# One load for the first keys, the second sketch matrix on GpSimd's queue, two banks for the last output tile, and a new order of all steps

## The chip, the cores and the metric

The kernel runs on one NeuronCore of a Trainium2 chip. The metric is the device time of one execution in microseconds, the median of a few runs; lower is better. Five engines work side by side and meet only at semaphores: TensorE (PE, matmuls), VectorE (DVE), ScalarE (ACT), GpSimd (POOL) and SyncE (SP, which here only starts transfers). Each takes its instructions strictly in the order in which they are written for it.

## The reference

An attention with sketched polynomial features feeds a layer with a rational activation. S is 1,088, there are 4 batches and 4 heads of 32 dimensions, and the output is 4,352 tokens of 128 values.

```python
def phi(x):                                   # 32 -> 64 features
    a = einsum('rd,bhsd->bhsr', S1, x); b = einsum('rd,bhsd->bhsr', S2, x)
    return einsum('bhsi,bhsj->bhsij', a, b).reshape(*x.shape[:-1], 64)
q_p, k_p = phi(q), phi(k)
kv  = einsum('bhsf,bhsd->bhfd', k_p, v);  z = sum(k_p, axis=2)
att = einsum('bhsf,bhfd->bhsd', q_p, kv) / (einsum('bhsf,bhf->bhs', q_p, z)[..., None] + 1e-6)
x = att.transpose(0, 2, 1, 3).reshape(4352, 128)
h = x @ w_in                                  # 128 -> 2048
P = a0 + a1*h + a2*h**2 + a3*h**3;  Q = 1 + |b0|*|h| + |b1|*h**2
out = (P / (Q + 1e-6)) @ w_out                # 2048 -> 128
```

## The kernel before

The whole program is one list of short steps, `ORDER`, read from left to right. Each step emits a few instructions on one engine, and an engine's queue is what the list gives to it, so the list alone sets the order of work on each engine. A letter behind the last dot picks the engine where there is a choice (`a` ScalarE, `d` VectorE).

Keys, `K<b>.<step>` for batch b: `T0`, `T1`, `T2` transpose parts of the keys on VectorE (L299), `s0`/`s1` sketch them on TensorE (L306), `c` copies one sketch out of PSUM, `f` multiplies the two sketches into features on VectorE (L318), `p0`/`p1` multiply the features with the values (L337, 72 matmul records in all), `k` keeps the result in `kvz`.

Queries, `Q<b>.<y>.<step>` for chunk y of batch b (256 to 384 tokens): `T` transposes, `sk` sketches, `c` copies the sketch, `dw` and `dr` write it to device memory and read it back repeated (SP), `f` makes the features, `p` multiplies with `kvz` (L433), `pl`, `r`, `x` divide, `b` transposes back on TensorE, `kk` copies the tokens into the ring `xT`. The first two chunks of batch 0 go without `dw` and `dr`.

The layer works in 21 units, each a number of tokens (256 or 512) by a number of blocks of 128 hidden values (4, 8 or 16), most of them 128 x 4,096 values. For unit i: `H<i>.<part>` the first matmul into a pair of PSUM banks (L518), `E` the cast out of them (ScalarE mostly, L272), `U` the absolute value, `W` and `Y` the denominator on VectorE (L531, L539, L554), in some units `D` (ScalarE) with `M` (an adding transfer from GpSimd), `P` and `V` the numerator (L559, L572), `A` an adding transfer, `L` and `X` logarithm and exponential on ScalarE (L576, L581), which make the reciprocal, `S` and `G` the products with it (L585, L589), and `Or`, `Os`, `Og` (and `Om`, `On` in units 16 and 17) the second matmuls (L618), which add into an output tile. `ST` copies that tile out of PSUM, `OUT` stores it. The last 256 tokens are units 18, 19 and 20.

`F<b>.k`, `.q`, `.v` load the next batch, `I<n>` are the loads at the start, `SS0` makes the sketch weights from S1 and S2 on VectorE (with some on GpSimd), `w`, `KA`, `AB`, `RT` prepare the weights and coefficients of the layer, `AW0` writes a constant. `Z<n>` is n idle matmuls of 128 x 512 that compute nothing (L197).

In PSUM a pool `att` has three banks (`att_ps`), `hps` two pairs (`h_ps`), and `ops` a single bank, `out_ps`, in which every output tile is built in turn. So the first `Or` of a tile waits until `ST` of the tile before has copied it out. In SBUF two buffers `out_sb` take the copies in turn; those of units 16 and 20 share one.

At the start, ScalarE's queue loads S1; SP loads the first 4 of the 9 key columns of each quarter (`I0`), S2 (`I11`), the other 5 columns (`I1`), half of the queries (`I2`), the values (`I3`, four transfers) and the rest. At the end `turn_out` of unit 20 copies one half of the last tile with VectorE and the other with ScalarE, and SP and ScalarE store one half each.

Of the kernel before, what the change touches and what calls it, by code (L numbers as in the profile page):

```python
# [43 lines left out]
Q0.1.b K1.p0 K1.p1 E2.1.a Q1.0.c.a w5.a Q0.1.kk.a L0.0 P2.0.d Q0.2.f Q0.2.p Q0.2.pl.a K1.k0.a X0.0 Q1.2.T U2.0.d
Q0.2.r Q1.1.sk Q1.2.sk Q0.3.dw F2.k Q1.0.dw Q0.2.x Q0.2.b Or0.0 W2.0.d S0.0 V2.0 K2.T0 G0.0 Y2.0 Q0.2.kk.a L1.0
Q1.1.c.a X1.0 H3.0 E3.0.a H3.1 E3.1.a K2.s0 K2.c0.a H3.2 L2.0 Q1.2.c.a E3.2.a F2.q Q0.3.dr Q1.1.dw S1.0 K2.T1 P3.0.d
G1.0 Q2.0.T K2.f0 Q2.1.T H3.3 E3.3.a Q0.3.f U3.0.d K2.T2 W3.0.d Q2.2.T Y3.0 Os0.0 H4.0 H4.1 Og0.0 Q2.0.sk Q1.0.dr
Q1.2.dw Q1.1.dr K2.s1 Q0.3.p X2.0 E4.0.a P3.1.a H4.2 Q0.3.pl.d K2.c1.d Q1.0.f Q2.0.c.a E4.1.a Og1.0 Q0.3.r V3.0 Q1.0.p
Q0.3.x L3.0 Q1.0.pl.a Q1.2.dr H4.3 E4.2.a Os1.0 Q1.0.r E4.3.a Q1.0.x Q0.3.b Q0.3.kk.a Q1.0.b Or2.0 S2.0 U4.0.d
Q1.0.kk.a H5.2 K2.f1 Q1.1.f W4.0.d X3.0 Q2.0.dw H5.3 E5.3.a G2.0 Q2.1.sk F2.v Q2.2.sk Q2.1.c.a F3.q E5.2.a Q1.1.p Y4.0  # L50
Q2.2.c.a Q1.1.pl.a Q1.1.r H5.0 E5.0.a Og2.0 L4.0 H5.1 Q1.2.f Or1.0 H6.2 Q1.1.x S3.0 E5.1.a Os2.0 ST2.a E6.2.a P4.0.d
Q3.1.T H6.3 Q1.1.b E6.3.a X4.0 Q1.1.kk.a H6.0 E6.0.a U5.0.d H6.1 Q3.0.T Q3.0.sk Q2.1.dw Q3.0.c.a W5.0.d E6.1.a K2.p0
K2.p1 K2.k0.a D6.0 Q1.2.p V4.0 Y5.0 S4.0 F3.k K3.T2 K3.T1 H7.0 K3.T0 E7.0.a U6.0.d G3.0 M6.0 Q1.2.pl.a Os4.0 H7.2
Or4.0 L5.0 E7.2.a H7.3 Q2.0.dr Q2.0.f Q2.0.p Q1.2.r Q2.1.dr Q2.1.f Q3.0.dw Q1.2.x X5.0 P5.0.d Q3.0.dr Q2.2.dw Q1.2.b
Q1.2.kk.a E7.3.a H7.1 Og3.0 G4.0 Q2.0.pl.d Q3.2.T E7.1.a Q2.0.r H8.3 V5.0 Q2.0.x Q2.0.b S5.0 L6.0 H8.2 E8.2.a U7.0.d
E8.3.a F3.v Or3.0 Q2.0.kk.a P6.0.d W7.0.d P7.0.d H8.0 V6.0 Os3.0 X6.0 Y7.0 E8.0.a S6.0 H8.1 E8.1.a U8.0.d D8.0 Q2.2.dr
OUT2 Og4.0 ST4.a H9.0 Q3.1.sk Q3.1.c.d Q2.2.f Q2.1.p Q2.1.pl.d K3.s0 K3.c0.d Q2.1.r Q3.2.sk Q3.2.c.d E9.0.a H9.1 Or6.0
L7.0 M8.0 Q2.1.x Q2.1.b K3.f0 H9.2 E9.1.a X7.0 E9.2.a Os6.0 H9.3 E9.3.a V7.0 AW0 Or5.0 P8.0.d H10.3 G6.0 L8.0 G5.0
S7.0 U9.0.d E10.3.a W9.0.d H10.0 E10.0.a V8.0 Q3.1.dw Y9.0 Og6.0 X8.0 H10.1 H10.2 Og5.0 E10.1.a A7.0 G7.0 E10.2.a
Q2.1.kk.a H11.0 Q3.1.dr Q3.1.f Os5.0 S8.0 D10.0 Q2.2.p E11.0.a U10.0.d P9.0.d K3.s1 Q2.2.pl.d ST6.a Q3.2.dw H11.1  # L60
Or8.0 Q3.0.f OUT6 Q2.2.r H11.2 K3.c1.d Q2.2.x L9.0 E11.1.a P10.0.d Q2.2.b K3.f1 V9.0 M10.0 V10.0 X9.0 E11.2.a H11.3
E11.3.a S9.0 K3.p0 K3.p1 w7.d U11.0.d w6.d L10.0 W11.0.d H12.1 E12.1.a Or7.0 H12.0 K3.k0.d Q3.0.p Q3.1.p X10.0 Y11.0
Q3.1.pl.d H12.2 Q3.0.pl.a G8.0 E12.0.a L11.0 E12.2.a Q3.0.r Os8.0 A9.0 H12.3 E12.3.a Q3.1.r Og8.0 Q3.0.x Q3.0.b Og7.0
Q3.1.x G9.0 Q2.2.kk.a S10.0 A10.0 Q3.0.kk.d H13.0 D12.0 Q3.1.b Q3.1.kk.a U12.0.d ST8.a M12.0 P12.0.d H13.1 E13.1.a
Q3.2.dr P11.0.d E13.0.a Or9.0 X11.0 H13.3 Q3.2.f V12.0 G10.0 V11.0 S11.0 H13.2 E13.3.a E13.2.a U13.0.d Or10.0 H14.1
E14.1.d L12.0 OUT4 Q3.2.p W13.0.d Q3.2.pl.a Q3.2.r H14.2 E14.2.d H14.0 X12.0 E14.0.a H14.3 Q3.2.x Q3.2.b Y13.0 E14.3.a
Q3.2.kk.a H15.2 D14.0 S12.0 U14.0.d A12.0 G12.0 E15.2.a Og10.0 Og9.0 ST10.a P14.0.d Z4 H15.3 P13.0.d L13.0 A11.0
Or12.0 G11.0 V14.0 V13.0 E15.3.a X13.0 S13.0 H15.1 Og11.0 E15.1.a H15.0 E15.0.a Or11.0 M14.0 U15.0.d L14.0 H16.1
P15.0.d W15.0.d OUT8 E16.1.a H16.0 E16.0.a Og12.0 X14.0 H16.3 ST12.a E16.3.a V15.0 OUT10 Y15.0 H16.2 S14.0 E16.2.a
Or13.0 U16.0.d A13.0 OUT12 G13.0 W16.0.d H17.3 H17.1 L15.0 Og13.0 E17.3.a A14.0 G14.0 Y16.0 E17.1.a X15.0 H17.0  # L70
E17.0.a S15.0 H17.2 E17.2.a U17.0.d L16.0 W17.0.d Og14.0 Or14.0 ST14.a A15.0 G15.0 H18.0 X16.0 Y17.0 S16.0 H18.1
E18.1.a E18.0.a Or15.0 U18.0.d B16.0 W18.0.d C16.0 Og15.0 H19.0 L17.0 X17.0 Os16.0 E19.0.a Y18.0 S17.0 Or16.0 Om16.0
# [7 lines left out]
def kernel(  # L80
# [63 lines left out]
        eng.dma_start(out=t, in_=bass.AP(tensor=s_in.tensor, offset=s_in.offset, ap=[[0, 16], [D, R], [1, D]]))  # L144
# [15 lines left out]
    qT0 = [ln_sb[:, 2048 + QW * i:2048 + QW * (i + 1)] for i in range(2)]  # L160

    def early(n):
        if n == 11:
            s_raw.append(spread_s(nc.sync, 1, S2))
        elif n < 2:
            j, e = ((0, 4), (4, NT))[n]
            nc.sync.dma_start(out=k0.rearrange("p (m t d) -> p m t d", m=NM, d=D)[:, :, j:e],
                              in_=bass.AP(tensor=k.tensor, offset=k.offset + j * D,
                                          ap=[[NJ * D, 128], [NT * D, NM], [1, (e - j) * D]]))
# [433 lines left out]
    def gather(i, y, k):  # L603
        t0, tl, f0, n = units[i]
        first = t0 not in outs
        if first:
            outs[t0] = ops.tile([128, TC], FP, name="out_ps")
        c, ce = span(i, "LSGGG"[y], k)
        for j, x in enumerate(range(c // tl, ce // tl)):
            left[t0] -= 1  # L610
            z = (live[i]["s3", 0][:, x * tl:(x + 1) * tl] if y == 4
                 else at(i, "rsgg"[y], x * tl, (x + 1) * tl))
            w = w_sb[y][:, f0 + x, :]
            if not (TOK or t0 + tl == n_tok):
                nc.tensor.matmul(outs[t0][:, :tl], lhsT=w, rhs=z, start=first and j == 0, stop=left[t0] == 0)
                continue
            for m in range(tl // 128):
                nc.tensor.matmul(outs[t0][:, m * 128:(m + 1) * 128],  # L618
                                 lhsT=z[:, m * 128:(m + 1) * 128], rhs=w,
                                 start=first and j == 0 and m == 0, stop=left[t0] == 0 and m == tl // 128 - 1)  # L620

    def turn_out(i, eng="d"):
# [10 lines left out]
        nc.vector.tensor_copy(out=o[:, 0:128], in_=outs[t0][:, 0:128])  # L633
# [1 line left out]
        nc.scalar.copy(out=last, in_=outs[t0][:, 128:256])
# [135 lines left out]
```

## Time and profile before

| | us |
|---|---|
| median of three runs | 254.69 (254.11 to 255.16) |
| the profiled execution | 254.41 |
| its span, first to last instruction | 252.6 |
| PE busy | 244.7 (97%) |
| VectorE busy | 240.3 (95%) |
| ScalarE busy | 229.2 (91%) |
| GpSimd busy | 31.2 (12%) |

The profile is one execution of the program. Its page gives busy times of the engines, slices of the span, the chain of waits that ended last, and the costliest groups of instructions. Behind the page stands the trace, which can be asked for the timeline of an engine, for busy times in any stretch, or for one tile. A row of a timeline is start, duration, engine, line, operation and shapes, and in brackets the idle time before it and what ended it. A busy matmul row is a modelled one, and rows that overlap are merged.

### The profile page before, as it was taken

The page shows a single profiled execution, that of the slowest core. Times are in us where ns is not written, and L with a number is a line of the kernel's source. Part 1 is how long each engine was busy: PE and PEld are TensorE (multiplying, and loading weights), DVE is VectorE, ACT ScalarE, POOL GpSimd, SP SyncE. Part 2 cuts the span into 40 slices and gives each one's busy share as a digit, 9 for nine tenths or more (in the row PEclk, how much of TensorE's full clock was granted, in tenths as well). Part 3 has the DMA queues.
Part 4 walks back from the last instruction along what each step waited for, and adds up shares of the span by engine and source line. Part 5 has one row for each costly group of instructions (what it writes and reads, how often), then busy time and mean ns, then how long its engine had stood idle before and what let it go on. Part 6 is the DMA issues. An engine that isn't in the chain of part 4 may idle for free.

```text
span 252.6 us, 6102 instructions
## 1 busy us (share of the span) xinstructions
PE 244.7 (97%) x2606; PEld 171.9 (68%) x2606; DVE 240.3 (95%) x231; ACT 229.2 (91%) x177; POOL 31.2 (12%) x59
## 2 busy tenths in 40 slices
...
DVE  2798999999999999999999999999999999999993
...
GB/s 164 277 328 210 126 241 197 131 100 257 174 20 156 188 195 77 87 197 192 4 42 168 180 236 79 115 190 195 44 197 57 200 210 91 29 16 3 42 23 21
DMA packets 22458, 34.47 MB, mean 136 GB/s; under 512 B 2976, under 2 KB 14880, under 8 KB 22432
## 3 DMA queue, kind: packets, MB, share of 16 engines
...
q8 instruction: 20, 0.33, 0.5%
q10 hardware_dynamic: 288, 0.08, 0.1%
...
## 4 chain that ended last, share of the span: by engine, by line
DVE 45%; PE 33%; issue 11%; DMA 6%; ACT 2%; SPq 1%; POOL 0%; DVEq 0%; ACTq 0%
PE h_ps L518 18%; PE out_ps L618 9%; DVE g L589 7%; DVE g L572 7%; DVE w L554 5%; DVE s L585 5%; DVE u L531 4%; DMA w<-u 4%; DVE g L559 4%; DVE w L539 3%; DMA v_sb<-in_v_dram 2%; PE att_ps L433 2%; DVE g L594 2%; PE att_ps L337 2%; DVE a_all L417 1%
## 5 line engine op out<-in xcount | busy, mean ns | idle before, releaser
L518 PE MATMUL h_ps<-xT,w_in_sb 128*128 128x512 f32 (+1 forms) x320 | 128.7, 539 | 0.1
L518 PEld LDWEIGHTS h_ps<-xT,w_in_sb 128*128 128x128 f32 x320 | 56.7, 190 | 36.6 <-issue 31.8
L272 ACT CAST hh<-h_ps 128x1024 bf16<-128x1024 f32 x66 | 66.6, 1047 | 3.3 <-PE h_ps L518 2.8
L581 ACT ACTIVATE r<-ln 128x4096 bf16<-128x4096 f32 (+2 forms) x21 | 63.1, 3005 | 0.4 <-ACT xT L272 0.3
L576 ACT ACTIVATE ln<-w 128x4096 f32<-128x4096 bf16 (+2 forms) x16 | 45.0, 2811 | 0.4 <-DVE w L554 0.4
L585 DVE TENSOR_TENSOR s<-hh,r 128x4096 bf16<-128x4096 bf16 (+2 forms) x21 | 39.5, 1881 | 0.0
L618 PEld LDWEIGHTS <-r 128*128 128x128 bf16 x544 | 31.8, 98 | 8.9 <-issue 8.6
L618 PEld LDWEIGHTS <-g 128*128 128x128 bf16 x544 | 31.6, 98 | 6.9 <-issue 6.0
L618 PE MATMUL out_ps<-w_out,r 128*128 128x128 bf16 x544 | 33.6, 219 | 1.2 <-ACT out_sb L272 1.1
L589 DVE TENSOR_TENSOR g<-g,s 128x4096 bf16<-128x4096 bf16 (+2 forms) x19 | 34.7, 1835 | 0.0
L572 DVE TENSOR_TENSOR g<-g,hh 128x4096 bf16<-128x4096 bf16 (+2 forms) x19 | 34.6, 1829 | 0.0
L618 PE MATMUL out_ps<-w_out,g 128*128 128x128 bf16 x480 | 29.7, 219 | 0.0
L554 DVE TENSOR_TENSOR w<-w,u 128x4096 bf16<-128x4096 bf16 (+2 forms) x16 | 28.0, 1750 | 0.0
L550 POOL DMA_DIRECT2D w<-u x10 | 9.3, 1026 | 131.0 <-ACT w L544 111.6
L618 PEld LDWEIGHTS <-s 128*128 128x128 bf16 x352 | 20.6, 98 | 4.7 <-issue 4.6
L531 DVE TENSOR_SCALAR u<-hh 128x4096 uint16<-128x4096 uint16 (+2 forms) x21 | 21.4, 1020 | 0.8 <-ACT hh L272 0.8
L568 POOL DMA_DIRECT2D g<-ones x16 | 16.8, 1452 | 26.2 <-DVE g L572 8.6
L544 ACT ACTIVATE w<-hh,root 128x4096 bf16<-128x4096 bf16 x5 | 18.9, 3773 | 0.0
L576 ACT ACTIVATE ln<-w,scale 128x4096 f32<-128x4096 bf16 x5 | 18.9, 3771 | 0.0
L559 DVE TENSOR_SCALAR g<-hh,a_k 128x4096 bf16<-128x4096 bf16 (+2 forms) x16 | 18.6, 1174 | 0.0
L618 PE MATMUL out_ps<-w_out,s 128*128 128x128 bf16 x288 | 18.0, 219 | 0.0
L539 DVE TENSOR_SCALAR w<-u,b_abs 128x4096 bf16<-128x4096 bf16 (+2 forms) x15 | 16.6, 1107 | 0.1
...
## 6 DMA issues: line engine op xcount, KB each, us to landing
g<-ones POOLq DMA_DIRECT2D x16, 512.0 KB, 10.4
...
```

The costliest lines, as they stand in the source:

```text
L272: nc.scalar.copy(out=out, in_=in_)
L518: nc.tensor.matmul(t[:, (x - part * m) * tl:(x - part * m + 1) * tl], lhsT=w_in_sb[:, (f0 + x) * 128:(f0 + x + 1) * 128], rhs=xT[:, p:p + ...
L531: nc.vector.tensor_scalar(out=at(i, "u", *c).bitcast(U16), in0=at(i, "hh", *c).bitcast(U16), scalar1=0x7FFF, scalar2=None, op0=AX.bitwise_and)
L539: nc.vector.tensor_scalar(out=at(i, "w", *c), in0=at(i, "u", *c), scalar1=ab1, scalar2=ab0, op0=AX.mult, op1=AX.add)
L554: nc.vector.tensor_mul(out=at(i, "w", *c), in0=at(i, "w", *c), in1=at(i, "u", *c))
L559: nc.vector.tensor_scalar(out=at(i, "g", *c), in0=at(i, "hh", *c), scalar1=a3, scalar2=a2, op0=AX.mult, op1=AX.add)
L572: nc.vector.tensor_mul(out=at(i, "g", *c), in0=at(i, "g", *c), in1=at(i, "hh", *c))
L576: nc.scalar.activation(out=ln_sb[:, :ce - c], in_=at(i, "w", c, ce), func=ACT.Ln, bias=1.0 + 1e-6, scale=scale0 if i in SQ else 1.0)
L581: nc.scalar.activation(out=at(i, "r", c, ce), in_=ln_sb[:, :ce - c], func=ACT.Exp, scale=-1.0)
L585: nc.vector.tensor_mul(out=at(i, "s", *c), in0=at(i, "hh", *c), in1=at(i, "r", *c))
L589: nc.vector.tensor_mul(out=at(i, "g", *c), in0=at(i, "g", *c), in1=at(i, "s", *c))
L618: nc.tensor.matmul(outs[t0][:, m * 128:(m + 1) * 128], lhsT=z[:, m * 128:(m + 1) * 128], rhs=w, start=first and j == 0 and m == 0, stop=le ...
```

## The change

- `I0` now loads all first keys in one transfer, 128 rows of 4,352 bytes. `I1` and `I11` are gone.
- S2 is loaded from GpSimd's queue at the very start of the program, ahead of GpSimd's memsets.
- The output tiles that begin in units 15 and 17 are built in banks of the pool `att`, and the last tile (units 18 to 20) in two of them, one for each 128 tokens. For the last tile the loop over the halves is now the outer one in each gather, and the two copies at the end read a bank each.
- `ORDER` is another list: the same steps without `I1` and `I11`, with other places, with `Z10 Z1 Z1` instead of `Z10 Z3 Z3 Z2 Z4`, and with eleven small steps on the other of the two engines. `SS0` stands at its head, before the transposes of the keys.

```diff
+LATE = (15, 16, 17)
-I0 I11 I1 I2 K0.T0 SS0 Z10 K0.s0 K0.T1 K0.T2 K0.c0.a K0.f0 Q0.0.T Z3 K0.s1 Z3 Q0.0.sk I3 K0.p0 I8 F1.k I7 I9 I4 I5
-K0.c1.a K0.f1 Q0.0.c.a Q0.0.f Q0.1.T K0.p1 K0.k0.d Q0.2.T K1.T0 Q0.1.sk Q0.0.p Q0.2.sk K1.s0 K1.T1 Q0.1.c.a Q0.0.pl.a
+SS0 I0 K0.T0 K0.T1 K0.T2 I2 I3 Z10 Z1 K0.s0 K0.c0.a Q0.0.T K0.s1 Z1 K0.f0 Q0.0.sk Q0.1.T K0.c1.a K0.f1 Q0.0.c.a I7
+Q0.2.T Q0.0.f F1.k K0.p0 K0.p1 K0.k0.a I8 KA0 Q0.1.sk Q0.1.c.a Q0.0.p Q0.2.sk Q0.0.pl.a I4 AB0 K1.T2 K1.T1 Q0.2.c.a
...
-L18.0 On16.0 ST16.a U19.0.d H20.0 OUT14 W19.0.a P19.0.d B17.0 V19.0 Or17.0 C17.0 X18.0 Y19.0 P18.0.a V18.0 OUT16
-E20.0.a U20.0.d Os17.0 S18.0 L19.0 W20.0.d X19.0 Om17.0 On17.0 S19.0 ST17.a Y20.0 Or18.0 Or19.0 Os19.0 Os18.0 G19.0
-P20.0.a G18.0 Og19.0 Og18.0 L20.0 X20.0 Or20.0 V20.0 OUT17 S20.0 G20.0 Os20.0 Og20.0 ST20 OUT20
+L18.0 On16.0 ST16.a B17.0 Or17.0 V19.0 C17.0 W19.0.a Y19.0 P18.0.a V18.0 Os17.0 H20.0 X18.0 Om17.0 Or18.0 E20.0.a
+U20.0.d On17.0 S18.0 W20.0.d L19.0 X19.0 Or19.0 S19.0 Os18.0 Y20.0 G19.0 G18.0 ST17.a P20.0.a V20.0 Os19.0 L20.0 X20.0
+Og19.0 Og18.0 S20.0 Or20.0 G20.0 Os20.0 OUT17 Og20.0 OUT16 ST20 OUT20
...
-    s_raw = [spread_s(nc.scalar, 0, S1)]
+    s_raw = [spread_s(nc.scalar, 0, S1), spread_s(nc.gpsimd, 1, S2)]
...
-        if n == 11:
-            s_raw.append(spread_s(nc.sync, 1, S2))
-        elif n < 2:
-            j, e = ((0, 4), (4, NT))[n]
-            nc.sync.dma_start(out=k0.rearrange("p (m t d) -> p m t d", m=NM, d=D)[:, :, j:e], in_=...)
+        if n == 0:
+            load_k(0)
...
         if first:
-            outs[t0] = ops.tile([128, TC], FP, name="out_ps")
+            if t0 + tl == n_tok:
+                outs[t0] = [att.tile([128, 512], FP, name="end_ps", tag="att_ps") for m in range(2)]
+            elif i in LATE:
+                outs[t0] = att.tile([128, TC], FP, name="end_ps", tag="att_ps")
+            else:
+                outs[t0] = ops.tile([128, TC], FP, name="out_ps")
...
+        if t0 + tl == n_tok:
+            left[t0] -= (ce - c) // tl
+            for m in range(2):
+                for j, x in enumerate(range(c // tl, ce // tl)):
+                    x0 = x * tl + m * 128
+                    z = live[i]["s3", 0][:, x0:x0 + 128] if y == 4 else at(i, "rsgg"[y], x0, x0 + 128)
+                    nc.tensor.matmul(outs[t0][m][:, :128], lhsT=z, rhs=w_sb[y][:, f0 + x, :], start=first and j == 0,
+                                     stop=left[t0] == 0 and j == (ce - c) // tl - 1)
+            return
...
-        nc.vector.tensor_copy(out=o[:, 0:128], in_=outs[t0][:, 0:128])
+        nc.vector.tensor_copy(out=o[:, 0:128], in_=outs[t0][0][:, :128])
...
-        nc.scalar.copy(out=last, in_=outs[t0][:, 128:256])
+        nc.scalar.copy(out=last, in_=outs[t0][1][:, :128])
```

More of the change, by code (lines that the diff above doesn't have):

```diff
@@ L38 @@
 ORDER = """
-I0 I11 I1 I2 K0.T0 SS0 Z10 K0.s0 K0.T1 K0.T2 K0.c0.a K0.f0 Q0.0.T Z3 K0.s1 Z3 Q0.0.sk I3 K0.p0 I8 F1.k I7 I9 I4 I5
-K0.c1.a K0.f1 Q0.0.c.a Q0.0.f Q0.1.T K0.p1 K0.k0.d Q0.2.T K1.T0 Q0.1.sk Q0.0.p Q0.2.sk K1.s0 K1.T1 Q0.1.c.a Q0.0.pl.a
-Q0.0.r Q0.0.x K1.T2 Q0.2.c.a Z2 Q0.0.b K1.s1 I6 I10 Q0.2.dw Q0.1.f K1.c0.a Q0.3.T Q0.0.kk.a H0.0 w2.d K1.f0 AB0 RT0
-w0.a KA0 KA1 KA2 w4.a K1.c1.d F1.q K1.f1 E0.0.a U0.0.d H1.0 Q0.3.sk E1.0.a F1.v Q0.2.dr Q0.1.p H2.0 P0.0.d Q0.3.c.d
-W0.0.d Q0.1.pl.d Y0.0 Q0.1.r U1.0.d Q1.0.T V0.0 Q0.1.x W1.0.d Q1.1.T w3.a P1.0.a E2.0.a w1.a Y1.0 V1.0 H2.1 Q1.0.sk
@@ L44 @@
[L44 to L72, printed above, removed]
-L18.0 On16.0 ST16.a U19.0.d H20.0 OUT14 W19.0.a P19.0.d B17.0 V19.0 Or17.0 C17.0 X18.0 Y19.0 P18.0.a V18.0 OUT16
@@ L74 @@
-E20.0.a U20.0.d Os17.0 S18.0 L19.0 W20.0.d X19.0 Om17.0 On17.0 S19.0 ST17.a Y20.0 Or18.0 Or19.0 Os19.0 Os18.0 G19.0
-P20.0.a G18.0 Og19.0 Og18.0 L20.0 X20.0 Or20.0 V20.0 OUT17 S20.0 G20.0 Os20.0 Og20.0 ST20 OUT20
+SS0 I0 K0.T0 K0.T1 K0.T2 I2 I3 Z10 Z1 K0.s0 K0.c0.a Q0.0.T K0.s1 Z1 K0.f0 Q0.0.sk Q0.1.T K0.c1.a K0.f1 Q0.0.c.a I7
+Q0.2.T Q0.0.f F1.k K0.p0 K0.p1 K0.k0.a I8 KA0 Q0.1.sk Q0.1.c.a Q0.0.p Q0.2.sk Q0.0.pl.a I4 AB0 K1.T2 K1.T1 Q0.2.c.a
+K1.T0 K1.s1 K1.c1.a Q0.0.r KA1 I9 Q0.0.x Q0.0.b K1.s0 Q0.0.kk.a Q0.3.T I5 H0.0 Q0.3.sk I6 Q0.1.f K1.c0.a w2.d Q0.2.dw
@@ new lines @@
+F1.q K1.f0 RT0 w0.a K1.f1 Q0.1.p Q0.1.pl.d E0.0.a KA2 Q0.3.c.a P0.0.d w4.a Q0.1.r U0.0.d Q0.1.x H1.0 E1.0.a Q0.1.b
+Q0.1.kk.a W0.0.d H2.0 P1.0.a Q1.2.T Y0.0 E2.0.a H2.1 L0.0 Q1.1.T U1.0.d F1.v E2.1.a Q1.0.T Q1.0.sk Q1.0.c.a X0.0
+W1.0.d V1.0 Q0.2.dr I10 V0.0 Q0.3.dw Y1.0 Q0.2.f U2.0.d P2.0.d F2.k K1.p0 K1.p1 K1.k0.d Q0.2.p Q0.2.pl.d Q0.2.r Q0.2.x
+Q1.1.sk Q1.0.dw S0.0 Q0.3.dr Q1.2.sk F2.q W2.0.d Or0.0 Q0.2.b Os0.0 w5.a w3.a Q0.2.kk.a H3.0 K2.T2 L1.0 K2.T1 Q1.2.c.a
+X1.0 H3.1 Q1.1.c.a E3.0.a w1.a E3.1.a K2.T0 K2.s0 G0.0 Y2.0 K2.c0.a L2.0 H3.3 H3.2 E3.3.a S1.0 E3.2.a G1.0 V2.0 X2.0
@@ new lines @@
+Q1.1.dw Og1.0 P3.0.d H4.1 E4.1.a Og0.0 Q0.3.f K2.f0 P3.1.a H4.0 E4.0.a Q2.2.T Q2.0.T Q2.0.sk K2.s1 U3.0.d Q2.1.T
+W3.0.d Y3.0 L3.0 Q0.3.p Q0.3.pl.d Q2.0.c.d Q0.3.r H4.2 Q1.0.dr Os1.0 Q1.0.f Q1.0.p Q0.3.x Q0.3.b Q1.1.dr H4.3 V3.0
+Q1.0.pl.a Q1.0.r Q1.2.dw Q1.1.f K2.c1.a Q0.3.kk.a Q2.1.sk Q1.0.x S2.0 Q1.0.b Or2.0 E4.2.a E4.3.a Q1.0.kk.a U4.0.d
+Q2.1.c.a Q2.0.dw H5.3 X3.0 Q1.2.dr G2.0 W4.0.d F3.k Q2.2.sk E5.3.a Q1.1.p Q1.1.pl.a K2.f1 Q2.2.c.a H5.2 E5.2.a Q2.0.dr
+H5.0 E5.0.a Or1.0 Y4.0 H5.1 L4.0 E5.1.a Q1.1.r Q1.2.f F3.q Og2.0 Q1.1.x Q2.0.f Q3.0.T Q3.1.T S3.0 H6.2 Os2.0 ST2.a
@@ new lines @@
+E6.2.a H6.3 E6.3.a Q1.1.b Q1.1.kk.a X4.0 H6.1 P4.0.d H6.0 E6.0.a U5.0.d E6.1.a Q3.2.T W5.0.d F2.v Q2.1.dw K2.p0 V4.0
+K2.p1 K2.k0.a Y5.0 K3.T2 K3.T1 Q3.0.sk Q3.0.c.a Q1.2.p Q3.1.sk Q2.0.p S4.0 Q2.0.pl.d H7.0 Q1.2.pl.d Or4.0 H7.2 D6.0
+U6.0.d Os4.0 Q2.0.r Q1.2.r E7.0.a H7.1 L5.0 E7.2.a Q2.1.dr Q2.0.x Q1.2.x K3.T0 P5.0.d Q1.2.b P6.0.d H7.3 M6.0 G3.0
+Og3.0 AW0 X5.0 Q1.2.kk.a E7.1.a H8.2 E7.3.a Q2.1.f G4.0 V5.0 S5.0 U7.0.d Q2.0.b L6.0 H8.3 E8.3.a E8.2.a P7.0.d Or3.0
+X6.0 W7.0.d H8.0 Q2.2.dw Q3.1.c.d H8.1 Os3.0 Y7.0 Og4.0 E8.0.a V6.0 E8.1.a Q2.0.kk.a H9.0 U8.0.d S6.0 G5.0 D8.0
```

21 lines of the change are left out of this document (17 added, 4 removed).

## The prediction, made before the changed kernel had run

> **What bounds the kernel now.** I read the page first (engine totals, slices, chain), then the busy time by windows, then the timelines of the first 20 us and of the last 12 us.
>
> ```profile
> PE 244.7 (97%) x2606; PEld 171.9 (68%) x2606; DVE 240.3 (95%) x231; ACT 229.2 (91%) x177; POOL 31.2 (12%) x59
> DVE  2798999999999999999999999999999999999993
> DVE 45%; PE 33%; issue 11%; DMA 6%; ACT 2%; SPq 1%; POOL 0%; DVEq 0%; ACTq 0%
> ```
>
> Three engines are almost full, so there is no single idle engine to exploit. The slices say where the holes are: in the first three and in the last. The windows give them in us (columns: window, its length, PE, PEld, DVE, ACT, POOL busy with instructions, clock, DMA share, GB/s):
>
> ```profile
> 0.00:10.00 10.00, 8.09 (x64) 3.77 (x64) 5.13 (x11) 2.22 (x4) 2.98 (x25) 1.00 0.82 191
> 10.00:20.00 10.00, 10.00 (x158) 8.18 (x160) 8.21 (x16) 5.26 (x14) 2.06 (x8) 1.00 1.03 327
> 20.00:30.00 10.00, 9.13 (x140) 7.16 (x138) 9.22 (x22) 9.89 (x14) 0.00 (x0) 1.00 0.62 171
> 30.00:240.00 210.00, 209.81 (x2124) 145.70 (x2123) 209.37 (x172) 205.42 (x141) 26.14 (x26) 1.00 0.58 130
> ```
>
> VectorE stands still 10 - 5.13 + 10 - 8.21 + 10 - 9.22 = 7.4 us in the first 30 us and only 0.63 us in the next 210. From 30 us on the kernel is a full VectorE (with a full TensorE beside it, where 10 of the 22 idle matmuls in its count are dropped by the change). A shorter kernel must come from VectorE getting its first steady work sooner, from less VectorE work, or from the end behind VectorE's last step.
>
> The front, on VectorE and then TensorE (start, duration, what; in brackets the wait before and who ended it):
>
> ```profile
> 3.79 0.71 DVE L299 STREAM_TRANSPOSE k_p<-k_sb 128x512 f32<-128x512 f32 x1 [2.67 <-DMA k_sb<-in_k_dram]
> 4.43 0.26 DVE L225 STREAM_TRANSPOSE sT<-s_raw 128x32 f32<-128x32 f32 x2
> 4.71 0.29 DVE L229 TENSOR_TENSOR S<-sT,mask 128x32 f32<-128x32 f32 x2
> 6.01 0.84 DVE L299 STREAM_TRANSPOSE k_p<-k_sb 128x384 f32<-128x384 f32 x2 [1.01 <-DMA k_sb<-in_k_dram]
> 6.77 1.19 DVE L318 TENSOR_TENSOR k_p<-h_ps,b_sk 128x1024 f32<-128x1024 f32 x1
> 7.88 0.42 DVE L366 STREAM_TRANSPOSE ln<-q_sb 128x256 f32<-128x256 f32 x1
> 8.23 1.45 DVE L318 TENSOR_TENSOR k_p<-h_ps,b_sk 128x1280 f32<-128x1280 f32 x1
> 12.34 0.30 DVE L274 COPY kvz<-att_ps 128x132 f32<-128x132 f32 x1 [1.06 <-PE att_ps L337]
> ```
>
> ```profile
> 1.18 3.70 PE L197 MATMUL out_ps<-idle 128*128 128x512 bf16 x10 [1.18 <-DVE idle L190]
> 5.06 0.69 PE L306 MATMUL h_ps<-S,k_p 128*64 128x64 f32 x16 [0.18 <-DVE S L229]
> 7.38 0.82 PE L197 MATMUL out_ps<-idle 128*128 128x512 bf16 x3
> 9.97 2.32 PE L337 MATMUL att_ps<-v_sb,k_p 128*64 128x64 f32 x72 [0.16 <-DMA v_sb<-in_v_dram]
> 12.22 1.13 PE L383 MATMUL h_ps<-ln,SAB 64*128 64x256 f32 x8
> 13.29 0.69 PE L433 MATMUL att_ps<-kvz,a_all 128*64 128x66 f32 x16
> 16.18 3.72 PE L518 MATMUL h_ps<-xT,w_in_sb 128*128 128x256 f32 x16
> ```
>
> Two loads hold the front: the second part of the keys (6.01) and the values (9.97), behind which stand the key products K0.p (to 12.29), Q0.1.sk, Q0.0.p and the first hidden layer H0 at 16.18.
>
> **Part 1: the keys in one load, S2 on GpSimd's queue.** The issues of before:
>
> ```profile
> 0.72 0.45 SPq L167 DMA_DIRECT2D k_sb<-in_k_dram  x1
> 1.24 0.67 SPq L144 DMA_DIRECT2D s_raw<-in_S_dram  x1
> 1.95 0.59 SPq L167 DMA_DIRECT2D k_sb<-in_k_dram  x1
> 3.12 1.86 SPq L138 DMA_DIRECT2D v_sb<-in_v_dram  x4
> ```
>
> Two issues leave SP's queue ahead of queries and values (0.67 + 0.59 = 1.26 us with their gaps), so the four issues of v move from 3.12 to about 1.8. In bytes: the two key pieces are 256 and 320 KB in runs of 512 and 640 B; the second took from 3.79 to 6.01, 336 KB with S2, about 150 GB/s. One load is 544 KB in rows of 4,352 B. The window 10 to 20 us, where long rows dominate, moved 327 GB/s, which makes 1.7 us of data. The first piece took 3.07 us from issue, of which 256 KB at 150 GB/s are 1.75, so 1.3 us are fixed: 0.72 + 1.3 + 1.7 = 3.7 us. Bounds: 3.79 (when not half of it had landed) and 6.01 (when all had, in small runs). I take 4.3, nearer to the low end, because rate and fixed part both point there.
>
> S2 now comes by GpSimd's software queue, and the new order puts SS0 ahead of K0.T0, so VectorE, in order, does nothing until S2 is there. No row shows a small load by that queue. The nearest:
>
> ```profile
> 77.71 1.98 POOL L550 DMA_DIRECT2D w<-u  x2 [59.05 <-ACT w L544]
> DMA to landing us min/median/max: 5.5/10.4/14.3
> ```
>
> Its issue takes about 1.0 us against SP's 0.67; the 512 KB transfers (second row: those into tile g) take at least 5.5. Low end: S2 on SP was taken by VectorE at 4.43 without a wait, at most 3.2 us after its issue; 0.72 + 3.2 + 0.4 = 4.3. High end: 0.72 + 5.5 = 6.2. I take 4.3, since 16 KB is nearest to the S2 row itself. The Trainium skill, "DMA: Bandwidth & Descriptors", section "Anatomy of one DMA", fits a software-queue DMA as about 2.0 us plus its bytes over 436 GB/s; by that S2 would land near 2.8 and only the keys would count, and no run here has shown it. The same page, section "Issuing engines are not separate DMA queues", speaks against a gain from the queue itself: all queues share the same 16 DMA engines, only the issuing time is saved.
>
> Working from 4.3: SS0 0.52 to 4.8; T0 0.64, T1 and T2 0.84 to 6.3; sketches s0 on PE 5.5 to 6.1, their copy 0.3 to 6.4; Q0.0.T 0.35 to 6.65; f0 1.1 to 7.8; Q0.1.T 0.35; f1 1.4 to 9.55. The values, issued 1.3 us sooner behind 2 us less of key traffic, land at 8 to 8.5 (bound above 9.97), so p0 runs behind Q0.0.sk, before f1 ends; p1, 40 of the 72 products, 1.3 us, ends at 10.85 instead of 12.29. From there the order of TensorE is that of before: Q0.1.sk, Q0.0.p, back to tokens, H0. Gain 1.44; I take 1.3, because VectorE has K1.T0 to T2 ahead of Q0.0.r and the key load k1 (issued 6.3 instead of 6.88) must not be late for these. If S2 or the keys land d us after 4.3, f1 and the gain move by d: between 1.9 (d = -0.5) and -0.5 (d = 1.9).
>
> **Part 2: idle matmuls.** Before 10 + 3 + 3 + 2 in the front and 4 near 182 us, after 10 + 1 + 1 in the front alone: 22 become 12. They fill TensorE's waits and nobody waits for them. Zero on VectorE's path; what it may cost is a rival below.
>
> **Part 3: the order from 20 to 240 us.** Same instructions, save engine swaps: six small steps go from VectorE to ScalarE, five the other way, each 0.15 to 0.4 us:
>
> ```profile
> 18.02 0.30 DVE L274 COPY b_sk<-att_ps 128x160 f32<-128x160 f32 x1
> L585 DVE TENSOR_TENSOR s<-hh,r 128x4096 bf16<-128x4096 bf16 (+2 forms) x21 | 39.5, 1881 | 0.0
> L531 DVE TENSOR_SCALAR u<-hh 128x4096 uint16<-128x4096 uint16 (+2 forms) x21 | 21.4, 1020 | 0.8 <-ACT hh L272 0.8
> ```
>
> Net about 0.2 us less for VectorE, with copies like the first row's counted at 0.2 to 0.3 us and the sums den at half of it. Laying VectorE's steps end to end at such row lengths, the work ahead of U4, U8, U12 and U16 is within 0.5, 2.1, 0.3 and 0.2 us of before, so the units keep their places. What moves far are attention steps: Q2.0.f 18 us and Q3.0.f 24 us earlier, Q3.1.f 13 later; their sketches were written long before in either order. On SP, AW0 and OUT2 change places with repeats of Q2 and Q3; the tightest by the written order is Q0.2.dr, 1.2 us of VectorE's work ahead of Q0.2.f where it was 6.7, though SP runs ahead of that text when its waits allow. So I add waits, not work. Bounds: -0.6 (all waits of before go) and +2.6 (the holes of 10 to 30 us once more, 1.79 + 0.78). I take +0.4, nearer to the first: ScalarE still has 210 - 205.4 = 4.6 us of slack in this stage, and TensorE gains some.
>
> **Part 4: the end.**
>
> ```profile
> 242.97 1.50 PE L618 MATMUL out_ps<-w_out,r 128*128 128x128 bf16 x24 [1.12 <-ACT out_sb L272]
> 248.13 0.62 PE L618 MATMUL out_ps<-w_out,g 128*128 128x128 bf16 x8
> 247.39 0.69 DVE L589 TENSOR_TENSOR g<-g,s 128x1024 bf16<-128x1024 bf16 x1
> 248.79 0.29 DVE L633 COPY out_sb<-out_ps 128x128 f32<-128x128 f32 x1 [0.71 <-PE out_ps L618]
> 249.12 0.27 ACT L635 COPY last<-out_ps 128x128 f32<-128x128 f32 x1 [2.49 <-DVE out_sb L633]
> 249.41 0.62 ACTq L647 DMA_DIRECT2D out_dram<-last  x1
> L655 SPq DMA_DIRECT2D out_dram<-out_sb x46: 315/448/1511, 91.3 to 244.2; - x46
> ```
>
> The single out_ps bank holds back 96 matmuls until ST17's copy; with att_ps banks they go as their inputs come. That alone gives nothing: G20 ends at 248.08 on VectorE and the pile had just cleared at 248.13. The two banks do give something: VectorE's copy can start after four of the last eight matmuls, and ScalarE's no longer stands behind VectorE's but behind the last matmul, 248.75 instead of 249.08. Gain 0.33. One new cover: OUT16 now follows OUT17 on SP, and ST20's copy reuses OUT16's buffer. OUT17 issued until 244.2 + 0.45; four more issues at 0.45 end at 246.5. By the last store (issued 249.41, span over at 252.6: at most 3.2 us from issue to landing) the fourth, issued from 246.0, lands by 249.2 at the latest; at two thirds of that, since the span's end holds more than a landing, by 248.2, before the copy at 248.6. I cost it at 0, at most 0.6.
>
> **Sum.** -1.3 - 0.2 + 0.4 - 0.33 = -1.4 us. The profiled execution took 254.41 us (span 252.6 and 1.8 around it), 0.3 under the median 254.69. So about 253.0 in such an execution, and 253.3 against the median.
>
> **Rivals.** (a) The front gains nothing: S2 by the software queue or the values set it. For: the 5.5 us row. Against: that row moves 32 times the bytes. At d = 1.9 the front is +0.5, and with the other terms (-0.2 + 0.4 - 0.33) the time is 255.1. Chance 0.15. (b) The new order waits more in the middle. For: 0.63 us of waits in 210 can hardly improve, and one late transfer on a full VectorE costs its whole delay. Against: the leads above. With +1.5 instead of +0.4 it is 254.4; this kind 0.15, and 0.08 for over 3.1 us, where it is slower than 255.96. (c) Slower: TensorE's clock. The first ten idle matmuls took 0.37 us each, the later three 0.27 with overlap: a slow start, then a faster rate. If the thinner front (Z1 for Z3) makes TensorE slow again between 7 and 13 us, Q0.0.sk, K0.p, Q0.1.sk and Q0.0.p (1.13 + 2.32 + 1.13 + 0.69 = 5.3 us) nearly double where they are on the path. Two thirds of that, 3.5 us, gives 256.8. It decides when TensorE idles for several us, which needs S2 late as well: from T0 at 4.8 the holes are under 1 us. Chance 0.12. The Trainium skill, "TensorE: Matmul & The Clock Gate", section "What's actually happening", has the clock halve only after an idle window of about 3.4 us; by that rule (c) does not happen unless S2 lands past 7 us. The profile's clock column reads 1.00 even in the slow first ten, so the durations must tell.
>
> **How the numbers follow.** A measurement of this kernel tells 0.5%, 1.27 us, from no change: 253.42 and 255.96 are the limits. Forecast 0.50 (its own range 252.0 to 253.4); (a) 0.15 and the mild (b) 0.15 make "same" 0.30; the strong (b) 0.08 and (c) 0.12 make "slower" 0.20. The low end, 251.7, is the front at -1.9 and the middle at -0.6 with the rest of the sum; the high end, 256.3, takes in (a) and (b) and leaves out most of (c), about 0.15 with what lies below.
>
> **What would show it.** After: SS0 and K0.T0 back to back near 4.3, no wait between T0 and f0's transposes; p1 ending near 10.9; H0 near 14.9; VectorE idle about 6 us in the first 30 instead of 7.4, and about 1 us from 30 to 240; ScalarE's last copy 0.25 us behind VectorE's last, not after it. Wrong, if VectorE's first instruction waits for S2 beyond 5 us, if the products run slower than 2.3 us, or if the middle loses over 1.5 us.

## The result and the profile after

The changed kernel is slower: median 257.27 us of six executions (255.74 to 259.8) against 254.72, ratio 1.0105 with a 95% interval of 1.0071 to 1.014. The ratio leaves out the slowest of the six, which lies over 1.5% above the fastest. Its executions spread more than those of before (254.11 to 255.16); the profiled one took 259.41, 2.1 above its median, so its rows show the places of the loss and not quite its size.

First the busy time by windows, columns as in the prediction:

```profile
0.00:10.00 10.00, 7.28 (x48) 3.59 (x48) 3.53 (x10) 1.72 (x3) 3.71 (x26) 1.00 0.70 179
10.00:20.00 10.00, 9.55 (x152) 7.66 (x152) 7.05 (x15) 3.31 (x13) 1.61 (x8) 1.00 0.66 213
20.00:30.00 10.00, 10.00 (x121) 8.44 (x122) 9.38 (x19) 9.41 (x14) 0.00 (x0) 1.00 1.01 259
30.00:240.00 210.00, 206.09 (x2099) 141.86 (x2096) 206.54 (x176) 203.73 (x140) 25.89 (x26) 1.00 0.60 130
```

VectorE idles 10.0 us in the first 30 (7.4 before) and 3.5 in the next 210 (0.6 before). Its work is 0.3 us less (240.0 for 240.3). 2.6 + 2.8 - 0.3 = 5.1 us, and the span grew by 5.0, from 252.6 to 257.6. So two places lost time. The timelines of VectorE (with GpSimd's issue of S2 ahead of it) and of TensorE show the first:

```profile
1.26 0.74 POOL L145 DMA_DIRECT2D s_raw<-in_S_dram x1 [0.83 <-POOLq L765]
5.15 0.21 DVE L221 STREAM_TRANSPOSE sT<-s_raw 128x32 f32<-128x32 f32 x1 [4.03 <-DMA s_raw<-in_S_dram]
6.48 0.21 DVE L221 STREAM_TRANSPOSE sT<-s_raw 128x32 f32<-128x32 f32 x1 [1.12 <-DMA s_raw<-in_S_dram]
6.84 1.42 DVE L295 STREAM_TRANSPOSE k_p<-k_sb 128x512 f32<-128x512 f32 x3
```

```profile
1.18 4.87 PE L193 MATMUL out_ps<-idle 128*128 128x512 bf16 x11 [1.18 <-DVE idle L186]
7.60 2.19 PE L302 MATMUL h_ps<-S,k_p 128*64 128x64 f32 x36 [1.55 <-DVE k_p L295]
10.43 2.08 PE L379 MATMUL h_ps<-ln,SAB 64*128 64x256 f32 x8
12.66 2.86 PE L333 MATMUL att_ps<-v_sb,k_p 128*64 128x64 f32 x72
19.29 1.99 PE L514 MATMUL h_ps<-xT,w_in_sb 128*128 128x256 f32 x8
```

S1, whose queue did not change, is there at 5.15 and S2 at 6.48, and only then do the key transposes follow. The same sketch matmuls (Q0.0.sk) that took 1.13 us take 2.08, the products 2.86 for 2.32, and H0 starts at 19.29 instead of 16.18. The second place stands at 62 to 67 us, in VectorE's timeline; behind it stand the issues of SP ahead of it:

```profile
65.44 0.96 DVE L413 TENSOR_TENSOR a_all<-a_all,b_all 128x768 f32<-128x768 f32 x1 [2.77 <-DMA sk_d<-sk_sb]
66.69 1.01 DVE L362 STREAM_TRANSPOSE q_sb<-q_sb 128x384 f32<-128x384 f32 x2 [0.28 <-DMA q_sb<-in_q_dram]
```

```profile
49.54 0.56 SPq L403 DMA_DIRECT2D a_all<-sk_d  x1
50.20 1.27 SPq L406 DMA_DIRECT2D b_all<-sk_d  x2
51.51 0.44 SPq L129 DMA_DIRECT2D k_sb<-in_k_dram  x1
52.06 0.55 SPq L403 DMA_DIRECT2D a_all<-sk_d  x1
52.66 1.94 SPq L406 DMA_DIRECT2D b_all<-sk_d  x2
57.01 0.33 SPq L133 DMA_DIRECT2D q_sb<-in_q_dram  x1
```

The transfers of that window, with KB each and the median us from issue to landing:

```profile
a_all<-sk_d SPq DMA_DIRECT2D x1, 384.0 KB, 10.4
```

The row at 65.44 is Q2.0.f, which VectorE reached at 62.67. Its operands were issued at 52.06 to 54.6, behind another repeat (Q1.2) and the key load of batch 3, and the first of three took 10.4 us. The bracket names a write into `sk_d`, but Q2.0.f reads only the three repeats; when the last of these landed, no view shows. In the kernel before, the same repeat was issued and used so:

```profile
58.85 0.55 SPq L407 DMA_DIRECT2D a_all<-sk_d  x1
78.71 0.95 DVE L417 TENSOR_TENSOR a_all<-a_all,b_all 128x768 f32<-128x768 f32 x1
```

So the change issues it 6.8 us sooner and asks for it 16.0 us sooner: the lead shrinks from 19.9 us to 10.6. The end, in the timeline of all engines (VectorE's last product and copy, ScalarE's last copy and its store):

```profile
252.54 0.69 DVE L585 TENSOR_TENSOR g<-g,s 128x1024 bf16<-128x1024 bf16 x1
253.72 0.29 DVE L643 COPY out_sb<-end_ps 128x128 f32<-128x128 f32 x1 [0.49 <-PE end_ps L616]
253.95 0.27 ACT L645 COPY last<-end_ps 128x128 f32<-128x128 f32 x1 [2.16 <-PE end_ps L616]
254.24 0.62 ACTq L657 DMA_DIRECT2D out_dram<-last  x1
```

Here the change does what it says: from the end of VectorE's product to ScalarE's store 1.0 us (253.23 to 254.24), before 1.33 (248.08 to 249.41).

### The profile page after: what moved, and what is told of

The parts are those of the page before. It is cut to its first block, busy times and chain, and to the rows that moved or that the text cites. A ratio compares the mean times of both kernels' runs of the same rounds, so it can differ in the third digit from the quotient of the medians.

```text
span 257.6 us, 6079 instructions
## 1 busy us (share of the span) xinstructions
PE 245.5 (95%) x2596; PEld 172.9 (67%) x2596; DVE 240.0 (93%) x231; ACT 229.3 (89%) x177; POOL 31.2 (12%) x60
## 4 chain that ended last, share of the span: by engine, by line
DVE 42%; PE 20%; issue 17%; DMA 16%; ACT 2%; SPq 1%; POOL 0%; DVEq 0%; ACTq 0%; POOLq 0%
PE h_ps L514 10%; DVE g L585 6%; DVE w L550 6%; DVE u L527 5%; DVE g L568 5%; DVE g L555 4%; DMA g<-ones 4%; DVE s L581 4%; DMA w<-u 4%; DMA q_sb<-in_q_dram 4%; PE out_ps L628 3%; DVE w L535 3%; DMA b_all<-sk_d 2%; DMA s_raw<-in_S_dram 2%; DVE g L590 2%
## 5 line engine op out<-in xcount | busy, mean ns | idle before, releaser
L628 PEld LDWEIGHTS <-r 128*128 128x128 bf16 x512 | 29.9, 98 | 8.2 <-issue 7.9
L628 PEld LDWEIGHTS <-g 128*128 128x128 bf16 x512 | 30.0, 98 | 6.7 <-issue 5.6
L628 PE MATMUL out_ps<-w_out,r 128*128 128x128 bf16 x416 | 25.7, 219 | 0.6 <-ACT out_sb L268 0.6
L628 PE MATMUL out_ps<-w_out,g 128*128 128x128 bf16 x416 | 25.7, 219 | 0.0
L546 POOL DMA_DIRECT2D w<-u x10 | 9.9, 1116 | 129.7 <-DVE rec L446 64.9
L628 PEld LDWEIGHTS <-s 128*128 128x128 bf16 x320 | 18.6, 98 | 4.7 <-issue 3.8
L564 POOL DMA_DIRECT2D g<-ones x16 | 16.0, 1400 | 33.5 <-PE out_ps L628 9.2
L413 DVE TENSOR_TENSOR a_all<-a_all,b_all 128x704 f32<-128x704 f32 (+3 forms) x11 | 9.5, 868 | 3.4 <-DMA sk_d<-sk_sb 2.8
```

The source lines that it names most:

```text
L628: nc.tensor.matmul(outs[t0][:, m * 128:(m + 1) * 128], lhsT=z[:, m * 128:(m + 1) * 128], rhs=w, start=first and j == 0 and m == 0, stop=le ...
```

## The experiments

Theory 1: what costs is S2 on the software queue together with SS0 at the head of VectorE's order. Theory 2: the long loads fill the DMA engines and hold back small loads on any queue. Theory 3 (M below): waits in the middle of the new order. Each ratio is to the kernel before on the same chip, with its 95% interval.

**The changed kernel with S2 on SP.**

```diff
-SS0 I0 K0.T0 K0.T1 K0.T2 I2 ...
+I0 I11 SS0 K0.T0 K0.T1 K0.T2 I2 ...       (I11 loads S2 on SP; GpSimd's load is gone)
```

> The changed kernel with S2 back on SP's queue, right behind the one key load. Theory 1 (the software queue holds S2 until 6.5 us and VectorE's order puts everything behind it): the first key transpose starts by 5.7 us instead of 6.84, the matmuls of the key products run at 2.3 us instead of 2.86, H0 starts at about 17 instead of 19.3, and the time falls by about 2 us from the changed kernel, to 255. Theory 2 (not the queue: the 16 DMA engines are full with the key load and small loads wait behind it on any queue, as S1 did until 5.15): S2 still lands after 6 us and the time stays within 0.7 us of the changed kernel. Theory 3 (the new order of the middle is what costs): the front improves and the time stays above 256.5.

0.9999 (0.9963 to 1.0035), median 255.01: as fast as the kernel before, so about all of the loss is gone.

VectorE's timeline:

```profile
5.26 0.55 DVE L223 STREAM_TRANSPOSE sT<-s_raw 128x32 f32<-128x32 f32 x2 [4.14 <-DMA s_raw<-in_S_dram]
62.11 0.96 DVE L415 TENSOR_TENSOR a_all<-a_all,b_all 128x768 f32<-128x768 f32 x1 [2.85 <-DMA sk_d<-sk_sb]
```

TensorE's:

```profile
6.71 1.27 PE L304 MATMUL h_ps<-S,k_p 128*64 128x64 f32 x36 [0.66 <-DVE k_p L297]
10.31 2.26 PE L335 MATMUL att_ps<-v_sb,k_p 128*64 128x64 f32 x72
16.34 1.99 PE L516 MATMUL h_ps<-xT,w_in_sb 128*128 128x256 f32 x8
```

S2 is there 1.2 us sooner, but H0 starts 2.95 sooner: the rest is the rate of TensorE, 1.27 us instead of 2.19 for the sketches. The transposes start at 5.95, later than the 5.7 I had asked for, since S1 and S2 come only at 5.26, which fits theory 2 in part. The edit does a second thing: S2's issue stands ahead of queries and values again, which SP issues at 1.91 and 2.53 instead of 1.19 and 1.65. The wait of Q2.0.f is there unchanged.

**The kernel before with S2 on GpSimd.**

```diff
-    s_raw = [spread_s(nc.scalar, 0, S1)]
+    s_raw = [spread_s(nc.scalar, 0, S1), spread_s(nc.gpsimd, 1, S2)]       (I11 dropped from ORDER)
```

> The kernel before with S2 alone moved to GpSimd's queue, its key load still in two parts and its own order (keys' first transpose ahead of the sketch weights). Theory 1: the sketch weights wait for S2 until about 6 us instead of starting at 4.43, TensorE's first sketches start near 6.6 instead of 5.06, H0 at 17.5 or later instead of 16.2, and the time rises by 1 to 2.5 us, to 256 to 257. Theory 2: S2 lands by 4.5 as on SP, because the first key part is short, and the time stays within 0.5 us of 254.7. Theory 3 (middle): no change.

0.9959 (0.9935 to 0.9983), not slower, and even 0.4% faster.

VectorE's timeline, then TensorE's:

```profile
5.47 0.21 DVE L225 STREAM_TRANSPOSE sT<-s_raw 128x32 f32<-128x32 f32 x1 [0.83 <-DMA s_raw<-in_S_dram]
10.02 2.26 PE L337 MATMUL att_ps<-v_sb,k_p 128*64 128x64 f32 x72
16.17 3.72 PE L518 MATMUL h_ps<-xT,w_in_sb 128*128 128x256 f32 x16
```

S2 is taken at 5.47, about one us later than before, and the sketches start at 5.96 instead of 5.06, but H0 at 16.17 as before. The kernel before had TensorE waiting for the values until 9.97; here it reaches the products at 10.02 without a wait, so that slack swallows the delay. Theory 1 in its bare form falls: this queue costs nothing where a cover lies over it. What the 0.4% comes from, the profile does not show.

**The changed kernel with more idle matmuls at its head.** Two sizes, to hold TensorE's rate up while S2 is awaited:

```diff
-... Z10 Z1 K0.s0 ...
+... Z26 Z1 K0.s0 ...          (second run: Z17)
```

> The changed kernel with 26 idle matmuls at its head instead of 10, so that TensorE stays busy until the first sketches come. If a slow TensorE clock after the hole from 6.05 to 7.6 us is part of the loss: the key products take 2.3 us instead of 2.86, Q0.0.sk 1.1 instead of 2.08, the products end near 13.8 instead of 15.5, and the time falls by 1 to 1.7 us to 255.6 to 256.3. If the clock plays no part (the sketch rows are long for another reason) the rows stay and the time is within 0.5 us of the changed kernel; if the extra idle matmuls themselves hold the sketches up, it is slower by the overrun.

> The changed kernel with 17 idle matmuls at its head instead of 10, to end near 7.4 us, before the sketches can start at 7.6, so that nothing is held up by them. In the runs so far H0 starts 11.1 us after VectorE takes S2 when the products run at 2.26 us, and 12.8 to 13.6 after it when they are slower. Clock theory: the products take 2.3 us, H0 starts 11.1 to 11.4 us after S2 is taken, and the time falls by 1 to 2 us, to about 256. Rival: the extra work on TensorE doesn't change when the sketches run; then H0 follows S2 by 12.5 us or more, or the time stays within 0.7 us of the changed kernel though it does not.

With 26: 1.0105 (1.006 to 1.015), no gain. The products run at 2.26, but S2 came at 7.25 in that profile and the idle matmuls ran until 8.8, past the first transpose. With 17: 1.008 (1.0053 to 1.0107), 256.45.

VectorE's timeline:

```profile
6.33 0.21 DVE L221 STREAM_TRANSPOSE sT<-s_raw 128x32 f32<-128x32 f32 x1 [0.96 <-DMA s_raw<-in_S_dram]
```

TensorE's:

```profile
7.45 1.27 PE L302 MATMUL h_ps<-S,k_p 128*64 128x64 f32 x36 [0.74 <-DVE k_p L295]
11.04 2.26 PE L333 MATMUL att_ps<-v_sb,k_p 128*64 128x64 f32 x72
17.08 1.99 PE L514 MATMUL h_ps<-xT,w_in_sb 128*128 128x256 f32 x8
```

H0 follows S2 by 10.75 us where it took 12.8, so the rate of TensorE is worth 2 us of the front. Of these the ratios show 0.6, and the interval overlaps that of the changed kernel. In the profile, an execution 2.1 us above its median, VectorE waited 2.3 us for queries and 2.1 for an adding transfer. The clock theory holds for the rows and falls for the time; that such transfer waits take the place of the gain in the other executions too is not shown.

**The kernel before with one key load.**

```diff
-I0 I11 I1 I2 K0.T0 ...     (I0: 4 of 9 columns, I1: 5)
+I0 I11 I2 K0.T0 ...        (I0: load_k(0))
```

> The kernel before with its first keys in one load instead of two and S2 on SP right behind them, its order otherwise its own. My prediction's step had the whole key load land at 4.3: then the first transpose waits until about 4.3 instead of 3.79, the second does not wait at 6.01, and the time is 0 to 0.8 us under before. Theory 2 (the long load holds the small ones back): the sketch weights wait until 5 us or later, the first sketches start at 5.7 or later instead of 5.06, and the time is 0 to 1 us over before.

0.9981 (0.9953 to 1.0009): no difference that the runs resolve.

VectorE's timeline, then TensorE's:

```profile
5.11 0.71 DVE L301 STREAM_TRANSPOSE k_p<-k_sb 128x512 f32<-128x512 f32 x1 [3.99 <-DMA k_sb<-in_k_dram]
10.42 2.27 PE L339 MATMUL att_ps<-v_sb,k_p 128*64 128x64 f32 x72
16.58 3.72 PE L520 MATMUL h_ps<-xT,w_in_sb 128*128 128x256 f32 x16
```

The first transpose starts at 5.11, not 4.3, the sketches at 6.37 instead of 5.06, H0 at 16.58. My figure for the landing was 0.8 us short. Of the 1.3 us that the sketches lose, 0.4 reach H0: the products follow at 10.42 without a wait, where before they had stood until 9.97 for the values.

**SS0 behind the key transposes, S2 still on GpSimd.**

```diff
-SS0 I0 K0.T0 K0.T1 K0.T2 I2 ...
+I0 K0.T0 K0.T1 K0.T2 SS0 I2 ...
```

> The changed kernel with S2 still on GpSimd's queue, but SS0 behind the three key transposes in VectorE's order. Theory 1a (it is the order, VectorE standing idle behind S2): the transposes run from about 4.5 to 6, SS0 at 6.5, TensorE's sketches begin at 7.1 instead of 7.6 and the time falls by 0.5 to 1.5 us. Theory 1b (it is S2's landing as such, since the sketches need both): H0 moves by no more than 0.6 us and the time by no more than 0.7.

1.0036 (1.0011 to 1.0061), 0.7% below the changed kernel (theory 1a).

VectorE's timeline:

```profile
4.88 1.43 DVE L295 STREAM_TRANSPOSE k_p<-k_sb 128x512 f32<-128x512 f32 x3 [3.76 <-DMA k_sb<-in_k_dram]
6.23 0.26 DVE L221 STREAM_TRANSPOSE sT<-s_raw 128x32 f32<-128x32 f32 x2
```

TensorE's:

```profile
6.86 1.27 PE L302 MATMUL h_ps<-S,k_p 128*64 128x64 f32 x36 [0.81 <-DVE S L225]
16.50 1.99 PE L514 MATMUL h_ps<-xT,w_in_sb 128*128 128x256 f32 x8
```

The transposes fill the wait, both S are there when they end, and H0 is at 16.50, near the 16.34 with S2 on SP. In time, moving one word of the order gives two thirds of what the other queue gave (0.7% of 1.06%), and the two intervals overlap.

**Three reads later in the middle; then together with each mend of the front.**

```diff
-... Q1.1.x Q2.0.f Q3.0.T Q3.1.T S3.0 ... U5.0.d E6.1.a ...
+... Q1.1.x S3.0 ... U5.0.d Q2.0.f Q3.0.T Q3.1.T E6.1.a ...
```

> The changed kernel with three steps of its order, Q2.0.f, Q3.0.T and Q3.1.T, moved behind U5.0, 4.6 us of VectorE's work later; the front stays as changed. Theory M (the new order asks for Q2.0's repeated sketches 2.8 us before they land, in front of a full VectorE, because two repeats, keys, queries and values of later batches all stand in the queues from 49 to 61 us): the wait of 2.8 us before Q2.0.f and that of 0.3 before Q3.0.T go, VectorE idles under 1 us from 30 to 240 instead of 3.5, and the time falls by 2 to 3 us from the changed kernel, to about 254.7. Rival N (that wait is covered: other waits come in its place, since TensorE is as full): idle stays at 2 us or more, and the time falls by less than 1 us.

> The changed kernel with both mends: S2 on SP's queue behind the keys, and Q2.0.f, Q3.0.T, Q3.1.T behind U5.0. If the front costs about 2.5 us and the middle about 2.8 us and they add, the time is 252 to 253, 2 us under before, which the tail's banks and 0.7 us of front account for. If they don't add (Rival N), it is 254 to 255, as with the first mend alone.

> The changed kernel with its loads, queues and banks as they are, and only the order mended: SS0 behind the three key transposes, and Q2.0.f, Q3.0.T, Q3.1.T behind U5.0. If the two places of the order add as the queue and the middle did (0.7% and 0.5% off the changed kernel's 1.0105), the ratio to before is 0.998, 254.0. If S2 on GpSimd's queue costs more than the order can hide, 1.003 or more.

Alone 1.005 (1.0023 to 1.0076), 255.5. With S2 on SP 0.9945 (0.9924 to 0.9965), 252.84. With SS0 behind the transposes 0.9975 (0.9957 to 0.9992), 253.74. Each is 0.5 to 0.6% below its partner without the three moves (1.0105, 0.9999, 1.0036), 1.4 us. Theory M had asked for 2 to 3: the wait of the profile goes, and half of its 2.8 us show in the time. It adds to the front: 1.06% and 0.55% make 1.61, and the two together measured 1.60. Q2.0.f in the first (alone) stands 15.1 us behind the issue of its repeat (53.09) and does not wait for it:

```profile
68.23 0.95 DVE L413 TENSOR_TENSOR a_all<-a_all,b_all 128x768 f32<-128x768 f32 x1
```

The windows of the first (alone) and the second (with S2 on SP):

```profile
10.00:20.00 10.00, 9.67 (x149) 8.05 (x149) 5.85 (x13) 2.59 (x8) 1.61 (x8) 0.69 0.63 199
30.00:240.00 210.00, 208.97 (x2147) 144.98 (x2142) 209.02 (x177) 206.61 (x143) 26.30 (x26) 1.00 0.61 131
```

```profile
20.00:30.00 10.00, 9.46 (x137) 7.63 (x136) 8.98 (x20) 8.88 (x12) 0.00 (x0) 1.00 0.81 222
30.00:240.00 210.00, 209.02 (x2130) 145.54 (x2128) 209.11 (x172) 206.09 (x141) 25.69 (x26) 1.00 0.60 128
```

VectorE's idle time from 30 to 240 is back at 1.0 and 0.9 us. The profile of the last (order only) has 2.7 us there, 1.8 of them before an adding transfer, and took 255.54 against its median of 253.74. A wait of that kind may be what sets this execution apart; the others left no trace. The second version is faster than both kernels. The third keeps every load, queue and bank of the change and moves four steps of the order, and it is 0.25% faster than the kernel before: the order is what made the change a loss. Whether the queue costs 0.3% beside it (0.9975 to 0.9945) the two overlapping intervals leave open.

**The banks alone, in the kernel before.** The edit is the gather, the two copies and LATE of the change, with the order of before.

> The kernel before with the banks of the change alone: tiles of units 15 and 17 and the two halves of the last in banks of att, its own order and front. My prediction: ScalarE's last copy starts about 0.25 us behind VectorE's instead of after it, 0.33 us sooner, the time 0.2 to 0.5 us under before. Rival: the banks of att make TensorE wait in a new place, and the time is 0.3 us or more over before.

0.9987 (0.9967 to 1.0007): 0.13%, 0.3 us, as forecast, though the interval includes no change. ScalarE's copy starts 0.23 us behind VectorE's.

**S2 ahead of the keys, in the version with both mends.**

```diff
-I0 I11 SS0 ...
+I11 I0 SS0 ...
```

> The version with both mends, with S2's load ahead of the key load on SP instead of behind it. If S2 and S1 wait behind the long rows of the keys in the DMA engines, both land by 4.2 us instead of 4.7 to 5.3; the keys are 0.7 us later, so the transposes start near 5 instead of 5.4, and the time falls by 0.3 to 0.5 us, to 252.4. If the keys are then what is late, no difference.

1.0026 (0.9995 to 1.0056), worse by 0.8% than keys first.

VectorE's timeline:

```profile
2.87 0.50 DVE L223 STREAM_TRANSPOSE sT<-s_raw 128x32 f32<-128x32 f32 x2 [1.75 <-DMA s_raw<-in_S_dram]
6.54 1.43 DVE L297 STREAM_TRANSPOSE k_p<-k_sb 128x512 f32<-128x512 f32 x3 [2.94 <-DMA k_sb<-in_k_dram]
```

TensorE's:

```profile
7.31 1.84 PE L304 MATMUL h_ps<-S,k_p 128*64 128x64 f32 x36 [2.03 <-DVE k_p L297]
```

S1 and S2 land early, as theory 2 said. But the keys, issued at 1.46 instead of 0.72, are taken at 6.54, where the three profiles in which VectorE waited for one key load issued first had 4.61, 4.88 and 5.11: 0.74 us later at the start, 1.4 to 1.9 later at the end. And TensorE, idle for 2 us, runs the sketches slowly again.

## Why the prediction was wrong

The forecast was 253.3 us, between 251.7 and 256.3; the median is 257.27. The bounds that the prediction gave its two uncertain terms (front 0.5 us late, middle +2.6), added up with its other two, make 257.3: the range stopped short of its own bounds.

- **The landing of S2 and the keys (part 1).** This step failed. I put both at 4.3 us with 6.2 as the high end for S2; VectorE took S2 at 6.48 (6.3 to 7.25 in the profiles with this queue and order), and the keys at 4.61 and 4.88 in the two profiles of these loads where they were awaited first. Of the 2.2 us by which S2 missed, 0.5 are its issue, which I had at 0.72 and the trace has at 1.26; 1.6 are the way from issue to VectorE, 5.2 us where I had 3.6. I had chosen the low end because 16 KB is little. The size was not the point: S1, as small and on its old queue, came at 5.15, and S1 and S2 were both taken from 2.87 to 3.4 once S2 was issued ahead of the keys. What holds the small loads back, the one long key load or the queries and values that SP now issues 1.4 to 1.5 us sooner, no run separates. For the keys I had 327 GB/s; all loads together moved 248 to 328 GB/s in each us from 2 to 7. The Trainium skill, "DMA: Bandwidth & Descriptors", section "Anatomy of one DMA", would have had S2 there near 2.8 by the prediction's estimate, or 3.3 from the true issue; the trace has 5.2 us from issue to landing (issue 1.26), and the measurement decides.
- **The front's sum.** By its own rule, d = 2.2 means a front 0.75 us late. It was 3.1. The rest is TensorE's slow rate, rival (c), which I held at 0.12, left out of the sum and tied to a hole of several us; in the changed kernel's profile a hole of 1.55 stood before the slow rows, and the version with 17 idle matmuls, with 0.74, had none. (a) and (c) were one chain and not two rivals: the late S2 makes the hole. My text said that (c) needs S2 late, and still gave the two separate chances.
- **The middle (part 3).** +0.4 in the sum; 2.8 in the profile, about 1.4 in the medians. The step that failed is the sentence on the attention steps that move far: that Q2.0's sketch was written early says nothing of when its repeat is back. Q2.0.f is reached 16.0 us sooner than before, but its transfer is issued only 6.8 us sooner, behind another repeat and a key load, and a lead of 10.6 us was too short. The pair that I named as tightest, Q0.2, waited 0.6.
- **VectorE's work and the end (parts 3 and 4)** were right: 0.3 us less work (forecast 0.2), 0.3 us from the banks (0.33). The copy at the end waits 0.49 us for TensorE both with OUT16 behind OUT17 and, in the banks-only kernel, in the old order of stores, so that swap cost nothing.
- **Idle matmuls (part 2)** were costed at zero on VectorE's path; with a late S2 seven more of them were worth 2 us of the front's rows, yet little of the time.

With both mends the time is 1.4 us under before, as much as the forecast for the change itself. That is luck: in that profile H0 starts 0.4 us sooner than before, not 1.3.
